# A new order for all steps from the 14th on, in a kernel of a state-space layer and a feed-forward network

## The chip, the cores and the metric

The kernel runs on one core of one Trainium2 chip. The metric is the time of one execution on the device in microseconds (us); lower is better. Unless a text says otherwise, a time is the median of several runs. The engines of a core are TensorE (PE in the profile; its weight loads are a row of their own, PEld), VectorE (DVE), ScalarE (ACT), GpSimd (POOL) and SyncE (SP), whose queue issues nearly all DMAs of this kernel. Each engine works through its own queue of instructions in the order of the program, and waits where an instruction needs what another engine hasn't finished.

## What is computed

A Mamba-2 layer over 4 batches, 8 heads, 768 positions, 32 channels for each head, and 16 states, worked in chunks of 32 positions, followed by an RMS norm and a feed-forward network with a SwiGLU gate on 3072 tokens of 256 channels.

```python
log_a = np.log(np.clip(a, 1e-06, 1.0))
for c in range(nc):                              # chunks of 32 positions
    cum = np.cumsum(la, axis=-1)                 # la: log_a of the chunk
    L = np.exp(cum[:, :, :, None] - cum[:, :, None, :]) * causal
    CB = np.einsum('bhin,bhjn->bhij', Cc, Bc)
    y_intra = np.einsum('bhij,bhjd->bhid', CB * L, xc)
    y_inter = np.einsum('bhin,bhnd->bhid', Cc, state) * np.exp(cum)[:, :, :, None]
    y[:, :, sl] = y_intra + y_inter
    state = decay_full[:, :, None, None] * state + np.sum(Bx, axis=2)
...
x = y.transpose(0, 2, 1, 3).reshape(3072, 256)
xn = x / np.sqrt(np.mean(x * x, axis=-1, keepdims=True) + 1e-06) * rms_g
g, val = xn @ w_gate, xn @ w_val                 # 256 x 1536 each
out = (g * (1.0 / (1.0 + np.exp(-g))) * val) @ w_out     # 1536 x 256
```

All inputs and outputs are 32-bit floats. The kernel takes the chunks in larger steps than the reference (64 or 128 positions), which gives the same sums.

## The kernel before, in words

The 3072 tokens go through in 6 blocks of 512 (two pairs of 256 positions each). For each block the kernel works out the Mamba-2 part, which gives y, then the norm, then the feed-forward part. All of it is cut into some 1,700 small **steps**, and one long string, `order` (from line 1306), lists them. The loop behind it (line 1477 on) takes the steps one by one and calls the function that stands for each. Since each engine runs its queue in program order, the string sets the queue of every engine at once: which matmul PE does next, which sum DVE does next, which transfer SP sends next. Steps of different blocks are interleaved in it, so that PE has products of one block to do while the other engines prepare the next.

A step reads `block:kind.numbers`. Behind a `/` stands the pair of PSUM banks that it takes (0, 1 or 2), behind a `*` a number of filler products for PE. Steps of block 0 have functions of their own (`first_kinds`), the others are found in `kinds` (from line 1280); a kind there can stand for work on a later block than its number says.

Those that matter here:

- `log4`, `la0`, `mid`, `mids`, `r`, `sums`, `exp`: logarithms of a, and the masks of decays L for the first pairs. `exp` runs on ACT, the products of L with B·C (`L.*`, line 638) on DVE.
- `row.k`, `rowe.k` (line 1192), `rowout.k` (line 1185): rows of decays for four chunks. `rowe` takes an exponential on ACT and sends the result to memory (`rowe<-e_sb`, line 1196); `rowout` sends the rows themselves.
- `dT.p` (line 563) fetches those decays from memory, spread over partitions (`dT<-rowe`, line 566), and `Td.p` (line 571) multiplies them on DVE into the transposed C.
- `g.*`, `gg.p` (lines 592 and 599): products of B and C for a pair, which need `Td`. `gg.p/s` takes a PSUM pair s. `A`, `S`: additions to the state and the states. `y.p/s` (lines 705, 714, 734): the outputs of a pair, in a PSUM pair s.
- `yt.p` and `sq.p`: y copied and squared by ACT out of its PSUM pair, which is free for another step after that (lines 824, 827, 789).
- `ms`, `rs`, `xn`, `tx`: the norm, its result xn, and differences of parts of xn.
- `fetch.k` (line 171): one of 18 pieces of the weights, up to 0.5 MB, into one of six buffers. Weights are converted on the way: `pow.k` (line 210, two instructions on ACT), `man.k` (line 221, DVE), `wt.k` (line 227, DVE). A buffer is free again when `pow` and `man` have read it. `fetch.12` and above belong to w_out.
- `early.*` (line 901) and `gate.f` (line 891): gate and value products of block 0 for the first f tiles, done plainly; `silu`, `hid` behind them.
- `P.k.j` (line 977): one product of a scheme that needs 7 products instead of 8 for a 2 × 2 split of the weights and tokens, for the j-th pair of tiles of the 1536 channels; four matmuls each. `take` copies out of PSUM on ACT (line 983), `C` adds on DVE (line 989), `silu` and `hid` follow on ACT and on DVE or POOL.
- `O.k.h` (line 1108): one of 20 products of a similar scheme for the output weights, with its sums `u` (DVE) and `up` (POOL; line 1076) ahead of it and its totals `w` (line 1139 on DVE, or on ACT) behind it. `put`: the result goes out.

ACT holds one set of function tables at a time. `functions(name)` (line 195) emits a load (lines 200 and 202) where the steps, in the order of the string, change from silu to exponential or logarithm or back. The steps `set`, `exps` and `table` do nothing but call it.

The lines that walk the string:

```python
    for step in order.split():
        step, _, slots = step.partition("/")
        blk, _, step = step.partition(":")
        step, _, filler = step.partition("*")
        fillers[:] = [int(filler)] if filler else []
        kind, *numbers = step.split(".")
        picks[:] = map(int, slots)
```

Of the kernel before, what the change touches and what calls it, by code (L numbers as in the profile page):

```python
# [1518 lines left out]
```

## Time and profile before

| | |
|---|---|
| median of 3 runs | 386.6 us (386.2 to 387.43) |
| the profiled execution | 387.79 us |
| its span (first to last instruction) | 386.0 us |
| granted clock of PE | 1.000 |
| HBM read and written | 23.68 MB and 3.74 MB |

The profile is one execution. Its page gives for each engine the busy time, its share of the span, and the number of instructions. The span is a little shorter than the execution's time, since something lies around it. Matmuls are pipelined and their ends are modelled, so a busy PE isn't PE at its peak. A chain of work is followed back from the last instruction to whatever released each step. Waits are listed by the line that waited and the line that released it; a view by windows gives the busy time of each engine in each stretch, and a view in order of time single instructions with what they waited for.

### The profile page before, as it was taken

The page shows a single profiled execution, that of the slowest core. Times are in us where ns is not written, and L with a number is a line of the kernel's source. Part 1 is how long each engine was busy: PE and PEld are TensorE (multiplying, and loading weights), DVE is VectorE, ACT ScalarE, POOL GpSimd, SP SyncE. Part 2 cuts the span into 40 slices and gives each one's busy share as a digit, 9 for nine tenths or more (in the row PEclk, how much of TensorE's full clock was granted, in tenths as well). Part 3 has the DMA queues.
Part 4 walks back from the last instruction along what each step waited for, and adds up shares of the span by engine and source line. Part 5 has one row for each costly group of instructions (what it writes and reads, how often), then busy time and mean ns, then how long its engine had stood idle before and what let it go on. Part 6 is the DMA issues. An engine that isn't in the chain of part 4 may idle for free.

```text
span 386.0 us, 9707 instructions
## 1 busy us (share of the span) xinstructions
PE 379.9 (98%) x3837; PEld 330.1 (85%) x3837; DVE 282.1 (73%) x632; ACT 219.7 (57%) x455; POOL 152.3 (39%) x171
## 2 busy tenths in 40 slices
PE   8999999999999999999999999999999999999997
PEld 5675478889988999888898988899888899888996
DVE  6895979999997989656688566578735677454675
ACT  2778767957698361776571446562474551555410
POOL 5022046536756554553475501463630046112131
PEclk9999999999999999999999999999999999999999
DMA  8888987574127044355134050000100000100001
GB/s 90 226 125 231 325 152 156 159 168 72 11 39 135 10 73 104 54 98 126 34 55 87 15 109 2 1 17 21 56 3 2 0 8 28 56 0 0 2 0 56
DMA packets 110084, 28.04 MB, mean 73 GB/s; under 512 B 94840, under 2 KB 107992, under 8 KB 110040
## 3 DMA queue, kind: packets, MB, share of 16 engines
q1 hardware_dynamic: 107960, 27.30, 33.4%
q8 instruction: 30, 0.49, 0.5%
q10 hardware_dynamic: 2080, 0.13, 0.4%
q14 instruction: 14, 0.11, 0.1%
HBM read 23.68 MB, written 3.74 MB: 71 GB/s over the span
## 4 chain that ended last, share of the span: by engine, by line
PE 92%; DMA 3%; DVE 1%; SPq 1%; ACT 1%; issue 1%; DVEq 0%
PE gate L977 30%; PE o L1108 23%; PE val L977 22%; PE y L734 3%; PE gate L891 3%; PE o L1009 3%; PE g L599 1%; DMA rowe<-e_sb 1%; PE gate L901 1%; DMA dT<-rowe 1%; PE e L460 1%; PE g L592 1%; DMA L<-rowd 1%; SPq L143 0%; PE idle L328 0%
## 5 line engine op out<-in xcount | busy, mean ns | idle before, releaser
L989 DVE TENSOR_TENSOR c<-val,p 128x512 f32<-128x512 f32 x99 | 67.6, 687 | 39.1 <-PE val L977 30.3
L983 ACT COPY p<-gate 128x512 f32<-128x512 f32 x99 | 56.9, 582 | 49.7 <-PE gate L977 46.6
L977 PE MATMUL gate<-tx,wgv 128*128 128x256 f32 x264 | 65.8, 380 | 0.0
L977 PEld LDWEIGHTS gate<-tx,wgv 128*128 128x128 f32 x264 | 49.4, 190 | 6.7 <-ACT p L983 0.2
L1002 POOL TENSOR_TENSOR hid<-c 128x256 f32<-128x256 f32 x31 | 24.3, 795 | 76.4 <-ACT c L208 73.7
L208 ACT ACTIVATE c<-c 128x256 f32<-128x256 f32 x99 | 39.0, 414 | 25.4 <-DVE c L989 25.1
L1108 PE MATMUL o<-two,hid 128*128 128x128 f32 x308 | 42.4, 276 | 0.0
L1139 DVE TENSOR_TENSOR ob<-ob,o 128x128 f32<-128x128 f32 (+1 forms) x116 | 31.1, 295 | 14.0 <-PE o L1108 9.6
L1108 PEld LDWEIGHTS o<-two,hid 128*128 128x128 f32 x308 | 39.1, 192 | 1.1 <-ACT ob L1135 0.2
L1002 DVE TENSOR_TENSOR hid<-c 128x256 f32<-128x256 f32 x68 | 30.1, 455 | 7.9 <-ACT c L208 7.5
L977 PE MATMUL val<-tx,sw 128*128 128x256 f32 x132 | 33.9, 381 | 0.0
L977 PE MATMUL val<-xn,sw 128*128 128x256 f32 x132 | 33.9, 379 | 0.0
L977 PE MATMUL val<-xn,wgv 128*128 128x256 f32 x132 | 33.5, 380 | 0.0
L977 PE MATMUL gate<-xn,wgv 128*128 128x256 f32 x132 | 33.2, 381 | 0.0
L977 PE MATMUL gate<-tx,sw 128*128 128x256 f32 x132 | 33.1, 379 | 0.0
L1076 POOL TENSOR_TENSOR s<-s,hid 128x512 f32<-128x512 f32 (+1 forms) x14 | 18.1, 1291 | 28.3 <-PE o L1108 24.8
L493 POOL TENSOR_SCALAR_AFFINE_SELECT L<-L 64x512 f32<-64x512 f32 x32 | 22.0, 686 | 14.8 <-ACT L L208 13.7
L977 PEld LDWEIGHTS val<-xn,wgv 128*128 128x128 f32 x132 | 24.9, 190 | 3.4
L977 PEld LDWEIGHTS val<-tx,sw 128*128 128x128 f32 x132 | 24.6, 190 | 3.7 <-issue 0.4
L977 PEld LDWEIGHTS gate<-tx,sw 128*128 128x128 f32 x132 | 24.8, 190 | 3.2
L1002 DVE TENSOR_TENSOR hid<-u,gate 128x256 f32<-128x256 f32 x33 | 13.6, 417 | 18.5 <-ACT u L208 18.5
L1076 POOL TENSOR_TENSOR s<-hid 128x512 f32<-128x512 f32 (+1 forms) x15 | 19.6, 1310 | 18.5 <-DVE hid L1002 14.3
(211 smaller groups left out, 729.2 us busy)
## 6 DMA issues: line engine op xcount, KB each, us to landing
L<-rowd SPq DMA_DIRECT2D x32, 128.0 KB, 3.1
xr<-in_x_dram SPq DMA_DIRECT2D x24, 128.0 KB, 3.3
wr<-in_moe_w_out_dram SPq DMA_DIRECT2D x6, 511.5 KB, 5.3
out_dram<-ob SPq DMA_DIRECT2D x23, 128.0 KB, 1.9
wr<-in_moe_w_gate_dram SPq DMA_DIRECT2D x5, 511.5 KB, 4.5
wr<-in_moe_w_val_dram SPq DMA_DIRECT2D x5, 511.5 KB, 5.6
br<-in_B_dram SPq DMA_DIRECT2D x23, 64.0 KB, 3.0
dT<-rowe SPq DMA_DIRECT2D x10, 128.0 KB
```

Source lines behind the costliest of these rows:

```text
L208: nc.scalar.activation(**operands)
L493: nc.gpsimd.affine_select(out=L[r], in_=L[r], pattern=[[0, L.shape[1]], [1, HC]], compare_op=ALU.is_ge, fill=0.0, base=0, channel_multipli ...
L734: nc.tensor.matmul(out=y[2 * k + u][rows, (2 * n + i) * HC:(2 * n + i + 1) * HC], start=(k, u, rows.start) not in opened, stop=True, skip_ ...
L891: nc.tensor.matmul(out=gv[:, k], lhsT=w[:, t, fs], rhs=xns[0][:, t], start=(t == 0), stop=(t == 1))
L977: nc.tensor.matmul(out=dst[:, half[w]], lhsT=lhsT, rhs=rhs, start=(k in (1, 2, 5) and w == 0), stop=True, skip_group_check=True)
L983: nc.scalar.copy(out=t, in_=Xs[j])
L989: nc.vector.tensor_tensor(out=t, in0=Zs[j], in1=a, op=ALU.add)
L1002: engine.tensor_tensor(out=hid[:, 2 * j + c // 10 - 1, c % 10 - 1], in0=u, in1=src[:, half[1]], op=ALU.mult)
L1009: nc.tensor.matmul(out=o, lhsT=hid[:, f, k // 2, (k % 2) * P:(k % 2 + 1) * P], rhs=wo[:, f], start=opens, stop=(f == NF // 2 - 1), skip_gr ...
L1076: engine.tensor_tensor(out=hidden_or_sum(o)[:, g], in0=hidden_or_sum(in0)[:, g], in1=hidden_or_sum(in1)[:, g], op=ALU.add if in1[0] == "+" ...
L1108: nc.tensor.matmul(out=Os[blk, b][:, place * P:(place + 1) * P], lhsT=hidden_or_sum(u)[:, g], rhs=rhs, start=(blk, b) not in opened, stop= ...
L1139: nc.vector.tensor_tensor(out=o, in0=o, in1=src, op=ALU.add if what[0] == "+" else ALU.subtract)
```

## The change

Only the string `order` is another. It holds the same steps, with the same PSUM pairs and fillers; the first 16 are the same, and so are the last seven. In between the new string is a permutation: the lead-in (block 0 up to its first P steps) has another order, and so has the interleaving of every later block. The table loads aren't steps: they follow from the order. In the part below the whole lead-in up to `0:y.3` is shown, then the places of one step, `0:exps`, and the ends.

```diff
     order = """
         0:warm 0:a 0:set 0:bc.0 0:ident 0:bc.1 0:bc2.1.1 0:ones 0:zeros 0:ident16 0:whole 0:kinks
-        0:idle.7 0:gcol 0:x.0 0:never 0:after 0:fetch.0 0:fetch.1 0:x.1 0:whole16 0:mask.0.0/0
-        0:part 0:hmask 0:upto 0:mid 0:mids 0:part2 0:aT 0:mask.1.1/2 0:la0 0:log4.0.4 0:upto2 0:r.0
-        0:fetch.2 0:head 0:sel 0:middles 0:after2 0:fetch.3 0:log4.4.2 0:log4.6.2 0:bc.3 0:tmask
-        0:parts.0 0:log 0:c*2 0:cx 0:mask.0.1/1 0:turn.0 0:Tb.0 0:T.0 0:d 0:dx 0:sums.0.1 0:sums.0.0
-        0:exp.0.1 0:never16 1:exps 0:exp.0.0 0:turn.1 0:scale.1.0 0:scale.1.1 0:last.1 0:cc
-        0:scale.0.0 0:scale.0.1 0:T.1 0:mean 0:g.0.1/1 0:Tt.1.0 0:g.0.0/0 0:Tt.1.1 0:L.0.1 0:L.0.0
-        0:sums.1.1 0:exp.1.1 0:row.1 0:rowout.1 0:man.0 0:bc.2 0:mask.1.0/1 0:sums.1.0 0:rowe.1
-        0:g.1.1/0 0:L.1.1 0:Tl.1 0:g.1.0/2 0:exp.1.0 0:L.1.0 0:fetch.4 0:last.0 0:Tl.0 0:fetch.7
-        0:dT.2 0:tok 0:tokout 0:A.1 0:A.0 0:S.0 0:S.1 0:pow.0 0:wt.0 0:y.0/1 0:sq.0 0:pow.1 0:y.1/2
-        0:sq.1 0:row.0 0:yt.0 0:man.1 0:wt.1 0:mask.3/1 0:rowe.0 0:yt.1 0:ydone.1 0:r.1 0:man.3
-        0:scale.3 0:eps 0:early.0.0/0 0:early.0.1 0:rowout.0 0:ms.0 0:parts.1 0:pow.3 0:pow.2 0:wt.3
-        0:rs.0 0:mask.2/2 0:scale.2 0:man.2 0:wt.2 0:sums.3 0:sums.2 0:exp.3 0:turn.2 0:T.2 0:Tt.2.0
-        0:xn.0 0:turn.3 0:norm.0 0:T.3 0:Tt.3.1 0:Tt.2.1 0:fetch.5 0:Tt.3.0 0:exp.2 0:Td.2
-        0:early.1.0/1 0:early.1.1 0:dT.3 0:man.4 0:table.1 0:x.2 0:norm.1 0:man.5 0:Td.3 0:silu.0
-        0:hid.0 0:pow.4 0:gate.2/0 0:txp.0.0 0:cw.0.0 0:gg.2/1 0:L.2.0 0:wt.4 0:man.7 0:pow.5 0:wt.5
-        0:L1.2.2 0:fetch.8 0:fetch.9 0:silu.2 0:hid.2 0:man.8 0:pow.8 0:wt.8 0:L1.2.3 0:gate.3/2
-        0:pow.7 0:gate.4/1 0:fetch.6 0:man.6 0:A.2 0:txp.0.1 0:silu.3 0:x.3 0:hid.3 0:pow.6
-        0:gate.5/0 0:tx.0.2 0:txp.0.3 0:fetch.11 0:wt.7 0:man.9 0:fetch.10 0:S.2 0:silu.4 0:pow.9
-        0:fetch.12 0:hid.4 0:bc.5 0:wt.6 0:cwp.3.0 0:wt.9 0:silu.5 0:hid.5 0:man.11 0:cw.3.1
-        0:cw.3.2 0:cw.4.0 0:fetch.13 0:silu.1 0:y.2/2 0:S.3 0:x.5 0:cwp.4.1 0:ydone.0 0:switch.1
-        0:P.2.3 0:bc.4 0:x.4 0:switch.0 0:pow.11 0:P.1.3 0:P.1.4 0:take.1.3 0:C.11.3 0:P.2.4 0:P.6.3
-        0:yt.2 0:sq.2 0:gg.3/2 0:take.1.4 0:silug.11.3 0:C.11.4 0:L.3.0 0:take.6.3 0:cwp.3.3 0:P.5.3
-        0:cwp.1.0 0:P.7.3 0:silug.11.4 0:P.6.4 0:take.7.3 0:P.5.4 0:P.4.3 0:hidgp.11.3 0:wt.11
-        0:L1.3.2 0:scale.5 0:L1.3.3 0:cwp.4.2 0:cwp.4.3 0:take.6.4 0:C.22.3 0:P.3.3 0:man.10
-        0:scale.4 0:pow.10 0:wt.10 0:silug.21.3 0:cwp.5.0 0:cwp.5.1 0:hidg.11.4 0:P.7.4 0:take.7.4
-        0:y.3/2 0:C.12.3 0:fetch.15 1:table 0:silug.22.3 0:hid.1 0:P.4.4 0:pow.12 0:silug.21.4
...
-        1:w.21 1:put.2 2:sq2.1.3 2:P.2.1 2:C.11.1 2:L1.3 2:take.6.1 2:P.7.1 2:take.6.0 2:P.7.0
-        2:take.7.0 0:exps 2:P.5.0 2:L1.2 2:C.22.0 2:L 2:P.5.1 2:take.7.1 2:P.4.0 2:silu.21.0
...
-        5:O.14.0 5:O.5.1 5:w.17 5:u.15 5:O.1.0 5:O.1.1 5:O.19.0 5:O.19.1 5:w.12 5:w.19 5:w.24 5:w.23
-        5:put.3 5:put.0 5:put.1 5:O.10.0 5:O.10.1 5:w.25 5:put.2.1 5:O.14.1 5:w.21 5:put.2.0
+        0:idle.7 0:gcol 0:x.0 0:never 0:upto 0:whole16 0:mask.0.0/0 0:x.1 0:fetch.0 0:fetch.3
+        0:fetch.1 0:aT 0:mask.1.1/2 0:part 0:part2 0:head 0:mean 0:mid 0:mids 0:la0 0:upto2 0:hmask
+        0:tmask 0:sel 0:after 0:after2 0:log4.0.4 0:r.0 0:middles 0:parts.0 0:log 0:c*2 0:cx
+        0:mask.0.1/1 0:turn.0 0:Tb.0 0:T.0 0:d 0:dx 0:scale.1.0 0:sums.0.1 0:log4.4.2 0:sums.0.0
+        0:exp.0.1 0:exp.0.0 0:turn.1 0:T.1 0:last.1 0:Tl.1 0:Tt.1.1 0:scale.0.1 0:scale.0.0
+        0:scale.1.1 0:g.0.1/1 0:never16 0:L.0.1 0:sums.1.1 0:g.0.0/0 0:L.0.0 0:cc 0:fetch.2 0:bc.2
+        0:log4.6.2 0:Tt.1.0 0:last.0 0:row.1 0:rowe.1 0:exp.1.1 0:bc.3 0:rowout.1 0:mask.1.0/1
+        0:Tl.0 0:sums.1.0 0:g.1.1/0 0:L.1.1 0:exp.1.0 0:g.1.0/2 0:L.1.0 0:tok 0:tokout 0:A.1 0:A.0
+        0:S.0 0:S.1 0:man.0 0:y.0/1 0:yt.0 0:pow.0 0:wt.0 0:man.3 0:y.1/2 0:yt.1 0:ydone.1 0:sq.0
+        0:pow.3 0:row.0 0:rowe.0 0:sq.1 1:exps 0:eps 0:r.1 0:parts.1 0:early.0.0/0 0:early.0.1
+        0:pow.1 0:fetch.4 0:dT.2 0:rowout.0 0:man.1 0:wt.1 0:fetch.5 0:cw.0.0 0:fetch.7 0:pow.2
+        0:man.2 0:ms.0 0:rs.0 0:xn.0 0:txp.0.0 0:norm.0 0:scale.2 0:wt.2 0:wt.3 0:txp.0.1 0:mask.2/2
+        0:mask.3/1 0:sums.3 0:exp.3 0:sums.2 0:exp.2 0:turn.2 0:T.2 0:Tt.2.0 0:Tt.2.1 1:table
+        0:early.1.0/1 0:turn.3 0:T.3 0:Tt.3.0 0:silu.0 0:Tt.3.1 0:man.4 0:hid.0 0:early.1.1 0:norm.1
+        0:Td.2 0:man.5 0:dT.3 0:Td.3 0:pow.4 0:gate.2/0 0:pow.5 0:wt.4 0:wt.5 0:gg.2/1 0:L.2.0
+        0:L1.2.3 0:scale.3 0:silu.2 0:hid.2 0:fetch.8 0:x.2 0:man.8 0:L1.2.2 0:pow.7 0:silu.1
+        0:pow.8 0:wt.8 0:man.7 0:wt.7 0:gate.3/2 0:silu.3 0:fetch.6 0:pow.6 0:tx.0.2 0:man.6 0:hid.3
+        0:wt.6 0:cwp.3.0 0:A.2 0:S.2 0:gate.4/1 0:fetch.9 0:pow.9 0:silu.4 0:fetch.11 0:pow.11
+        0:cw.3.1 0:hid.4 0:man.9 0:man.11 0:wt.9 0:cwp.1.0 0:cw.4.0 0:cwp.4.2 0:gate.5/0 0:silu.5
+        0:table.1 0:hid.5 0:ydone.0 0:switch.1 0:x.3 0:y.2/2 0:S.3 0:cw.3.2 0:fetch.12 0:pow.12
+        0:yt.2 0:sq2.2.0.0 0:bc.4 0:wt.11 0:fetch.10 0:man.10 0:switch.0 0:P.1.3 0:take.1.3 0:P.1.4
+        0:P.2.3 0:C.11.3 0:txp.0.3 0:sq.2 0:hid.1 0:gg.3/2 0:P.6.3 0:P.2.4 0:silug.11.3 0:take.1.4
+        0:P.5.3 0:take.6.3 0:P.7.3 0:cwp.4.1 0:P.6.4 0:L1.3.3 0:man.12 0:C.11.4 0:P.5.4 0:bc.5 0:x.5
+        0:L1.3.2 0:scale.5 0:scale.4 0:spread.10 0:spread.9 0:sq2.2.1.3 0:spread.11 0:x.4 0:fetch.17
+        0:pow.10 0:wt.10 0:take.7.3 0:P.4.3 0:cwp.3.3 0:C.22.3 0:P.3.3 0:take.6.4 0:P.7.4 0:cwp.5.0
+        0:cwp.5.2 0:hidgp.11.3 0:cwp.5.1 0:L.3.0 0:y.3/2 0:silug.21.3 0:cw.1.1 0:C.12.3 0:silug.12.3
...
+        1:C.22.5 1:hidp.22.4 1:u.0 1:O.15.0 1:silu.11.5 1:hid.11.5 1:P.4.5 1:silu.21.5 1:hid.21.5
+        1:up.3 1:u.1 1:O.2.0 1:O.2.1 1:w.0 0:exps 1:P.3.5 1:C.12.5 1:L1.2 1:L 1:O.15.1 1:O.3.0
+        1:O.3.1 1:silu.12.5 1:hid.12.5 1:up.4 1:up.5 1:up.6 1:O.0.0 1:O.0.1 1:u.9 1:O.16.0 1:w.2
...
+        5:O.1.0 5:O.1.1 5:O.19.0 5:O.19.1 5:w.12 5:w.19 5:w.24 5:w.23 5:put.3 5:put.0 5:put.1
+        5:O.10.0 5:O.10.1 5:w.25 5:put.2.1 5:O.14.1 5:w.21 5:put.2.0
```

More of the change, by code (lines that the diff above doesn't have):

```diff
@@ new lines @@
+        0:put.3 1:T.1.0 0:w.23 1:hid.21.2 1:sq2.0.3 1:sq2.0.1 1:dT.1 0:put.1 2:bc.0 0:O.10 0:w.25
+        1:sq2.0.0 0:put.0 1:sq2.0.2 1:sq2.1.1 0:put.2 1:P.5.2 1:C.22.2 1:P.7.3 1:Tt.1.1 1:g
+        0:table.0 1:take.7.3 1:P.4.3 1:hidp.22.1 1:cwp.2.3 1:P.3.2 1:silu.22.0 1:hidp.22.0
+        1:silu.22.2 1:hidp.22.2 1:silu.21.3 1:C.11.3 0:sub.10 1:hidp.12.1 0:ex.10 1:P.1.4 1:take.1.4
+        1:hid.21.3 1:Td.0 1:C.12.2 0:sub.8 0:ex.8 1:silu.12.2 1:hidp.12.2 1:subp.2 1:Td.1 1:P.5.3
+        1:P.2.4 1:P.6.4 1:take.6.4 1:P.1.5 1:C.11.4 1:silu.11.4 1:take.1.5 1:C.22.3 1:silu.22.3
@@ new lines @@
+        2:C.11.4 2:hid.11.5 2:sub.1 3:Tt.1.0 2:silu.11.4 3:Td.1 2:P.7.5 2:take.7.5 2:P.7.4
+        2:take.7.4 2:P.5.4 2:hid.11.4 2:C.22.4 2:table 2:silu.22.2 2:hid.22.2 2:silu.22.4
+        2:hidp.22.4 2:P.4.5 2:silu.21.5 2:hid.21.5 2:up.1 2:P.4.4 2:silu.21.4 2:hid.21.4 2:yt
+        2:P.5.5 2:C.22.5 2:silu.22.5 2:up.0 2:u.3 2:up.4 2:hid.22.5 2:O.2.0 2:O.2.1 2:O.15.0
+        2:O.15.1 2:P.3.5 2:w.2 2:w.0 2:C.12.5 2:O.3.0 2:O.0.0 2:O.3.1 2:P.3.4 2:O.0.1 2:silu.12.5
+        2:hid.12.5 2:up.5 2:up.6 2:u.2 2:exps 2:ex.1 2:C.12.4 2:w.4 2:w.10 2:u.9 4:dT.1 3:spread.2
@@ new lines @@
+        4:O.10.0 4:O.1.1 4:O.10.1 4:w.25 4:w.17 4:put.3 4:put.0 4:w.21 4:w.14 4:put.2 4:w.23 4:w.19
+        4:put.1 5:P.6.1 4:exps 5:take.6.1 5:P.1.0 5:take.1.0 5:P.2.1 5:C.11.1 5:P.7.1 5:take.7.1
+        5:P.2.0 5:C.11.0 5:P.6.0 5:take.6.0 5:P.4.1 5:P.5.1 5:C.22.1 5:silu.21.1 5:hid.21.1 5:P.5.0
+        5:P.7.0 5:take.7.0 5:silu.11.0 5:P.1.3 5:take.1.3 5:P.3.1 5:C.12.1 5:silu.12.1 5:hidp.12.1
+        5:hid.11.0 5:P.4.0 5:silu.21.0 5:hid.21.0 5:P.6.3 5:take.6.3 5:C.22.0 5:silu.22.0
+        5:silu.11.1 5:hid.22.0 5:P.2.3 5:C.11.3 5:silu.11.3 5:silu.22.1 5:hid.22.1 5:P.1.2
```

258 lines of the change are left out of this document (120 added, 138 removed).

## The prediction

> **What bounds the kernel now.** I read the page's first part, then what TensorE waited for, then the windows of 10 us, and then the chain in order of time where a window was short of 10.
>
> ```profile
> span 386.0 us, 9707 instructions
> ```
>
> ```profile
> PE 379.9 (98%) x3837; PEld 330.1 (85%) x3837; DVE 282.1 (73%) x632; ACT 219.7 (57%) x455; POOL 152.3 (39%) x171
> ```
>
> TensorE (PE) is busy for 379.9 us, 98% of the span. A permutation keeps its matmuls, so only the other 2% are to be won from idle time. The next view, the waits of PE, says where it stood waiting for another engine behind the very start; the columns are total, times and longest, in us.
>
> ```profile
> PE g L599 <- DVE T L573: 0.7, 1, 0.7
> PE y L705 <- DVE S L686: 0.5, 1, 0.5
> PE o L1108 <- POOL s L1076: 0.4, 1, 0.4
> PE y L734 <- DVE L L632: 0.2, 1, 0.2
> ```
>
> They add to 1.8 us. The windows (stretch: length, busy time of PE, PEld, DVE, ACT, POOL with instructions; then PE clock, DMA share, GB/s) put them in their places.
>
> ```profile
> 0.00:10.00 10.00, 8.76 (x55) 5.73 (x57) 6.67 (x31) 3.16 (x8) 5.01 (x17) 1.00 0.81 92
> 10.00:20.00 10.00, 9.35 (x172) 6.38 (x170) 8.75 (x19) 8.02 (x15) 0.00 (x0) 1.00 0.87 234
> 30.00:40.00 10.00, 9.26 (x59) 5.36 (x58) 6.04 (x14) 7.32 (x12) 1.74 (x3) 1.00 0.85 238
> 40.00:50.00 10.00, 10.00 (x124) 4.50 (x126) 8.49 (x21) 7.50 (x12) 1.12 (x1) 1.00 1.02 279
> 120.00:130.00 10.00, 10.00 (x56) 8.99 (x55) 8.91 (x18) 5.09 (x13) 3.53 (x4) 1.00 0.53 73
> 200.00:210.00 10.00, 9.36 (x237) 8.48 (x239) 8.88 (x20) 1.86 (x6) 7.54 (x8) 1.00 0.53 105
> ```
>
> PE loses 1.24 us in the first window (most of it before anything has been loaded, and the first 16 steps are the same in both orders), 0.65 in the second, 0.74 between 30 and 40, and 0.64 between 200 and 210, which is the pair of waits of 0.4 and 0.2. The stretch 40 to 50 is full for PE, but its DMA share is 1.02: transfers queue there. That is all a new order has to work on, apart from new waits of its own. The granted clock is 1.00 in each of these windows.
>
> **The change part by part.** All products, sums, copies and transfers are kept, so I cost only places where PE waits now or would wait next.
>
> *The wait at gg.2 (30 to 40 us).* First the instruction that makes the decays, then the chain behind it (start, duration, what).
>
> ```profile
> 21.80 0.27 ACT L208 ACTIVATE e_sb<-r_ps 128x128 f32<-128x128 f32 x1
> ```
>
> ```profile
> 28.98 4.52 DMA rowe<-e_sb
> ...
> 33.55 3.35 DMA dT<-rowe
> ...
> 37.47 0.65 PE g L599 x20
> 38.13 7.06 PE gate L891 x16
> ```
>
> The decays of rowe.0 are ready at 22.07, but the queue of SyncE (SP) sends them at 28.98, behind fetch.4, fetch.7 and dT.2 among others. Two transfers in a row then bring dT.3 (33.55 + 3.35 = 36.90), VectorE (DVE) multiplies, and the second part of gg.2 starts 0.57 behind the landing, at 37.47. In the new order rowe.0 stands directly behind rowout.1 and ahead of fetch.4, dT.2 and fetch.7, and bc.2 has gone ahead of rowe.1. The cut is at least the stretch from the old fetch.4 to the old rowe.0.
>
> ```profile
> 26.20 0.43 SPq L184 DMA_DIRECT2D wr<-in_moe_w_gate_dram  x1
> ...
> 43.14 0.41 SPq L184 DMA_DIRECT2D wr<-in_moe_w_out_dram  x1
> ```
>
> So rowe.0 goes out 28.98 − 26.20 = 2.8 us earlier, and dT.3 lands near 36.90 − 2.8 = 34.1. PE comes to the second part of gg.2 when gate.2 and the first part are done; it stood waiting 0.74 there, so it wants it at 36.73. With those 0.57 behind the landing the multiplication is done by 34.7, in time by 2 us. **Gain 0.74**, the whole wait, and no more: late next is gate.2 itself.
>
> *The lead-in before it.* The steps from the logarithms to the first states are reordered among themselves. On DVE `head` and `mean` now stand ahead of `la0`, and on ScalarE (ACT) a logarithm, `log4.4.2`, directly ahead of the first mask exponential. By my walk through both queues with the old durations, gate.2 starts 0.2 later. No row shows the new order, so I bound this by the nearest wait that could vanish, and the nearest instruction that could come to stand in front.
>
> ```profile
> 16.02 2.35 DVE L638 TENSOR_TENSOR L<-g,L 128x1024 f32<-128x1024 f32 x2 [0.77 <-PE g L592]
> ```
>
> DVE, whose two mask products per pair set the pace here, idles 0.77 before the second pair: a better order gains up to 0.77. One of those products in the wrong place costs half of the 2.35 for two, 1.18. I take **+0.2 later**, near the middle.
>
> *The new place of gg.3 (50 to 55 us).* The stretch from gg.2 to the end of y.2 keeps its work (three gates, the state additions, y.2), so all of it comes 0.74 − 0.2 = 0.54 earlier. Behind y.2 stood five P steps and then gg.3; now there are three, and two of the five (P.6.3, P.2.4) follow it. gg.3 takes the PSUM pair that y.2 filled, so it waits until ACT has emptied it by yt.2 and sq.2. The chain shows what PE has to cover this with.
>
> ```profile
> 50.70 1.06 PE val L977 x4
> 51.76 1.73 PE gate L977 x8
> 53.48 0.86 PE val L977 x4
> 54.35 0.86 PE gate L977 x4
> 55.21 0.62 PE g L599 x32
> ```
>
> The first of them starts where y.2 ends. Five P steps were 1.06 + 1.73 + 0.86 + 0.86 = 4.51. Three are 1.06 + 0.86 + 0.86 = 2.78, so PE asks for gg.3 at 50.70 − 0.54 + 2.78 = 52.94. ACT's rows for that stretch before:
>
> ```profile
> 49.22 0.60 ACT L208 ACTIVATE u<-gate 128x512 f32<-128x512 f32 x1 [1.99 <-PE gate L891]
> 49.71 0.62 ACT L208 ACTIVATE u<-u 128x512 f32<-128x512 f32 x1
> 50.23 0.77 ACT L208 ACTIVATE e<-wr,kinks 128x512 f32<-128x512 int16 x1
> 51.03 0.72 ACT L208 ACTIVATE e<-e,kinks 128x512 int32<-128x512 f32 x1
> 52.66 0.58 ACT L983 COPY p<-gate 128x512 f32<-128x512 f32 x1 [0.90 <-PE gate L977]
> 53.14 0.44 ACT L824 COPY yt<-y 128x128 f32<-128x128 f32 x2
> ...
> 54.35 0.72 ACT L208 ACTIVATE sq<-y 128x128 f32<-128x128 f32 x3
> ```
>
> The last of these ends at 55.07 and gg.3 starts at 55.21, so already now there is no slack. In the new order ACT has silu.5, pow.12, yt.2, take.1.3, sq.2. silu.5 starts 0.54 earlier at 48.68; the next can start 0.49 behind it (49.71 − 49.22), at 49.17. pow.12 takes 51.03 + 0.72 − 50.23 = 1.52, to 50.69; yt.2 takes 54.35 − 53.14 = 1.21, to 51.90; take.1.3 takes 0.48, to 52.38; sq.2 takes 0.72, to 53.10; and 0.14 later, at 53.24, gg.3 starts. PE waits 53.24 − 52.94 = **0.3**, and every P step behind gg.3 in its queue waits with it.
>
> *Two more table loads.* The instructions are not quite kept: a table load is emitted where the set of functions changes in program order. Followed through both orders, there are 26 before and 28 after: `0:exps` now stands between products of block 1, near 128 us, with a silu soon behind it.
>
> ```profile
> 196.34 1.28 ACT L200 ACT_TABLE_LOAD   x1
> 197.63 0.42 ACT L208 ACTIVATE c<-c 128x256 f32<-128x256 f32 x1
> ```
>
> That is 2 × 1.28 = 2.56 us of ACT, in a window (120 to 130) in which ACT is busy for 5.09 of 10. I cost it at nothing; what hides it is the 4.91 idle, and with that gone it costs up to 2.56. Here a rule speaks against the change. The rows above show the next activation 0.01 us behind the end of the load. The Trainium skill, page "ScalarE: Activation LUTs", section "What ACT_TABLE_LOAD costs", gives 1283 ns for a load, as this trace does, but adds a drain of about 1380 ns; by it the pair would take some 5.3 us of ACT, by estimate 0.4 more than is idle, and the sum would come out 0.4 higher. No drain is seen in these rows behind the load, and I stay with 2.56.
>
> *Blocks 1 to 5.* PE does not wait there except for 0.64 near 205, where exponentials on ACT, POOL's masks and a sum on POOL come together. The same steps stand at that boundary in the new order. I cost it at nothing, bounded by −0.64 and, for as many new waits, +0.64. The last seven steps are the same, so the end behind the last product stays.
>
> *The sum* against the profiled execution, which took 387.79 us with a span of 386.0 (1.8 us lie around it, and it stands 1.2 us over the median of 386.6): −0.74 + 0.2 + 0.3 = −0.24, so 387.55 there, and 386.36 by the median; I say 386.4. A measurement of this kernel can tell about 0.3%, or 1.16 us, from no change: faster means under 385.44, slower over 387.76.
>
> **The rivals.** *First, more is won.* If the lead-in gains its 0.77 where I take a loss of 0.2, ACT is just in time for gg.3, and the new interleaving closes the 0.64 near 205, then −0.74 − 0.77 − 0.64 = −2.15, or **384.45**. For it: every one of these is a wait on one chain that an order can loosen, and nearly all steps of the lead-in have moved. Against it: each needs its own luck, and the lead-in has been walked without finding it.
>
> *Second, ACT blocks behind a fetch; slower.* pow.12 stood far behind y.3 before; now it stands ahead of yt.2 in ACT's queue, and it can't start before fetch.12 has landed. The first rows here are the waits of the SP queue for conversions on ACT, the last the mean time from issue to landing.
>
> ```profile
> SPq L184 <- ACT e L208: 6.5, 5, 2.8
> ```
>
> ```profile
> wr<-in_moe_w_out_dram SPq DMA_DIRECT2D x6, 511.5 KB, 5.3
> ```
>
> With the old issue at 43.14 it lands at 48.4, and ACT wants it at 49.17: 0.7 to spare. But this fetch takes a buffer that a conversion has to release, and such a wait was up to 2.8 us. Then it lands at 51.2, 2.1 late; yt.2, sq.2 and gg.3 are late by as much, and all of PE behind them: 386.36 + 2.1 = **388.4**. The point from which it decides: from a landing at 49.17 on, each us of lateness is a us of PE, and from 49.17 + 1.41 = 50.6 on the kernel is slower than the limit below. For it: the DMA share of 1.02 in just that stretch. Against it: in the new SP queue fetch.12 has gone ahead of fetch.10, so 0.5 MB less is in front of it.
>
> *Third, PE has far more room.* The weight loads (PEld) are busy for 85%, and 15% of 386 us would be 58 us. The trace speaks against it: from 21 us on the P steps follow each other at 0.86 us for four products and never faster, and PE waits only where the list says. If even a tenth of this were open to an order, the time would be **380.8**. The Trainium skill, page "Perfetto Trace Analysis", section "Identifying the Most-Contended Engine", holds that busy time of matmuls misleads and that the share of weight loads measures the headroom; on this kernel the constant pitch disagrees.
>
> *Fourth, the change doesn't quite do what it says.* Table loads and new waits at the block boundaries cost 0.64 at the old boundary's size up to 2.56 if ACT has no cover near 128 us: **387.0 to 388.9**.
>
> **How the numbers follow.** My forecast has 0.42 (of it 0.36 within the limit, 0.03 each beyond it); the first rival 0.29, the second 0.18, the third 0.03, the fourth 0.08 (0.05 within the limit, 0.03 slower). Faster: 0.03 + 0.29 + 0.03 = 0.35. Same: 0.36 + 0.05 = 0.41. Slower: 0.03 + 0.18 + 0.03 = 0.24. The range goes from the first rival's 384.4 to the second's 388.5. As both signs have much of the chance, the forecast's own range: from −0.77 instead of +0.2 in the lead-in to +1.18, which is 385.4 to 387.3.
>
> **What would show it.** In the changed profile: rowe's transfer starting near 26 and not 29, dT.3 landing near 34, and no wait of gg.2 for DVE at L573 (step one); gate.2 near 33.0 (lead-in); the last gate of block 0 ending 0.5 earlier; gg.3 near 53.2 with ACT's sq as its releaser and a wait of 0.3; 28 table loads and no PE wait between 120 and 140. PE's busy time should again be about 380. I am wrong if gg.3 waits for over 1.7 us with pow.12 behind a DMA (second rival), if windows of blocks 1 to 5 show PE under 9.9 in new places (fourth), or if the time falls although the list of waits is the same, which would mean that products ran at another pitch.

## The result, and the profile after

The changed kernel took 388.56 us (median of 7 runs, 388.04 to 390.42) against 386.63 us for the kernel before (7 runs). The measured ratio of the two, which need not be the quotient of the medians (1.0050 here), is 1.0061, with a 95% interval from 1.0039 to 1.0083: slower by more than the 0.3% that a measurement can tell, where 386.4 us and most likely no change was forecast. A second measurement of the same kernel, among the experiments, gave 389.94 us and 1.0083 (1.0062 to 1.0105). Five executions in what follows took 556 to 2205 us, one of them the profiled one of the first experiment (granted clock 0.657); the ratios and the readings of profiles leave them out.

The two strings are the same in their first 16 and their last 28 steps, so the new order begins with the 17th step, and not with the 14th as the title has it.

The profiled execution took 390.1 us. Its page, first and busy part:

```profile
span 388.4 us, 9717 instructions
```

```profile
PE 380.9 (98%) x3837; PEld 330.4 (85%) x3837; DVE 283.8 (73%) x632; ACT 223.4 (58%) x457; POOL 149.4 (38%) x171
```

The span is 2.4 us longer. PE's busy time grew by 1.0 us only, and the products are the same, so most of it is waiting. What PE waited for (total, times, longest, in us):

```profile
PE y L664 <- DMA xr<-in_x_dram: 1.3, 2, 0.8
PE idle L328 <- DVE warm L354: 1.1, 1, 1.1
PE o L1108 <- DVE s L1076: 0.9, 1, 0.9
PE gate L977 <- DVE xn L873: 0.4, 1, 0.4
PE o L1108 <- DVE ob L1139: 0.4, 1, 0.4
PE gate L977 <- DVE hid L924: 0.2, 1, 0.2
```

The wait of `gg.2` (L599 behind DVE, L573) is gone from this profile, as forecast. In its place stand one for a load of x, and three at a block boundary. The windows (columns as in the prediction) show where:

```profile
10.00:20.00 10.00, 9.81 (x168) 7.00 (x170) 8.46 (x19) 7.16 (x14) 0.00 (x0) 1.00 0.92 242
30.00:40.00 10.00, 10.00 (x64) 5.82 (x64) 8.78 (x18) 9.35 (x17) 0.72 (x1) 1.00 0.80 212
...
60.00:70.00 10.00, 8.72 (x181) 6.78 (x180) 7.06 (x19) 5.76 (x16) 5.49 (x7) 1.00 0.90 223
120.00:130.00 10.00, 10.00 (x54) 8.87 (x53) 8.58 (x17) 6.17 (x15) 4.11 (x5) 1.00 0.46 64
190.00:200.00 10.00, 9.12 (x182) 8.21 (x181) 7.60 (x15) 8.10 (x15) 8.09 (x7) 1.00 0.27 60
200.00:210.00 10.00, 9.15 (x74) 8.36 (x72) 8.67 (x16) 2.65 (x8) 5.65 (x7) 1.00 0.21 46
```

30 to 40 is full now (9.26 before). 60 to 70 has lost 1.28, and 190 to 210 has lost 1.73 where it lost 0.64 before.

**The load.** In SP's queue `x.4` now stands behind `spread.10`, `spread.9`, `sq2.2.1.3` and `spread.11`, eight transfers. The chain of the changed kernel in order of time:

```profile
58.41 0.50 SPq L500
...
60.47 3.82 DMA xr<-in_x_dram
64.30 0.04 issue
64.34 0.66 PE y L664 x40
```

The second half of `x.4` is sent at 60.47 and has landed at 64.30. The additions to the states that `y.3` makes for the next two pairs (L664) start there, in the middle of `y.3`, and every P step queues behind them.

**The boundary of blocks 2 and 3.** First before, then after (start, duration, what):

```profile
194.87 1.18 DVE L1076 TENSOR_TENSOR s<-s,hid 128x512 f32<-128x512 f32 x1
...
196.61 0.71 PE L1108 MATMUL o<-wo,hid 128*128 128x128 f32 x4
197.16 0.61 PE L1108 MATMUL o<-sw,s 128*128 128x128 f32 x4
```

```profile
194.33 1.28 ACT L202 ACT_TABLE_LOAD   x1
...
196.46 0.29 DVE L1139 TENSOR_TENSOR ob<-ob,o 128x128 f32<-128x128 f32 x1 [0.48 <-ACT ob L208]
196.66 1.75 DVE L1076 TENSOR_TENSOR s<-s,hid 128x512 f32<-128x512 f32 x1
...
198.55 0.68 PE L1108 MATMUL o<-sw,s 128*128 128x128 f32 x4 [0.88 <-DVE s L1076]
```

The sum `u.9` (DVE, L1076) stood ahead of the totals `w.4` and `w.10`. Now it stands behind them, and `w.10` waits for a copy that ACT makes only behind its table load. So `u.9` ends near 198.4 and not at 196.05, in a kernel that is 1.0 us later here as a whole (`3:g` at 196.47 and 195.47). PE asks for `O.9.0` (`o<-sw,s`) directly behind the products of `3:g`, where the old order had `O.4.0` (`o<-wo,hid`) first, and waits 0.88.

### The profile page after: what moved, and what is told of

The parts are those of the page before. It is cut to its first block, busy times and chain, and to the rows that moved or that the text cites. A ratio compares the mean times of both kernels' runs of the same rounds, so it can differ in the third digit from the quotient of the medians.

```text
span 388.4 us, 9717 instructions
## 1 busy us (share of the span) xinstructions
PE 380.9 (98%) x3837; PEld 330.4 (85%) x3837; DVE 283.8 (73%) x632; ACT 223.4 (58%) x457; POOL 149.4 (38%) x171
## 4 chain that ended last, share of the span: by engine, by line
PE 84%; DVE 5%; DMA 5%; SPq 2%; ACT 1%; issue 1%; POOL 1%; POOLq 0%; DVEq 0%; ACTq 0%
PE gate L977 28%; PE o L1108 23%; PE val L977 21%; PE o L1009 3%; PE y L734 2%; DMA wr<-in_moe_w_gate_dram 2%; DMA wr<-in_moe_w_val_dram 2%; PE g L599 1%; DMA xr<-in_x_dram 1%; PE gate L901 1%; SPq L500 1%; DVE S L688 1%; PE g L592 1%; DVE hid L1076 1%; ACT e L208 1%
## 5 line engine op out<-in xcount | busy, mean ns | idle before, releaser
L989 DVE TENSOR_TENSOR c<-val,p 128x512 f32<-128x512 f32 x99 | 67.2, 686 | 42.9 <-PE val L977 30.6
L977 PE MATMUL gate<-tx,wgv 128*128 128x256 f32 x264 | 65.6, 380 | 0.0
L977 PEld LDWEIGHTS gate<-tx,wgv 128*128 128x128 f32 x264 | 49.4, 190 | 6.8 <-issue 0.2
L1002 POOL TENSOR_TENSOR hid<-c 128x256 f32<-128x256 f32 x31 | 23.7, 771 | 77.8 <-ACT c L208 77.6
L1002 DVE TENSOR_TENSOR hid<-c 128x256 f32<-128x256 f32 x68 | 30.6, 460 | 9.3 <-ACT c L208 9.2
L977 PE MATMUL val<-xn,sw 128*128 128x256 f32 x132 | 34.1, 381 | 0.0
L977 PE MATMUL gate<-xn,wgv 128*128 128x256 f32 x132 | 33.5, 382 | 0.6 <-DVE xn L873 0.4
L977 PE MATMUL val<-tx,sw 128*128 128x256 f32 x132 | 33.4, 379 | 0.0
L977 PE MATMUL val<-xn,wgv 128*128 128x256 f32 x132 | 33.4, 379 | 0.0
L977 PE MATMUL gate<-tx,sw 128*128 128x256 f32 x132 | 32.9, 380 | 0.0
L1076 POOL TENSOR_TENSOR s<-hid 128x512 f32<-128x512 f32 (+1 forms) x15 | 19.7, 1314 | 24.2 <-DVE hid L1002 21.8
L1076 POOL TENSOR_TENSOR s<-s,hid 128x512 f32<-128x512 f32 (+1 forms) x14 | 17.2, 1228 | 28.2 <-PE o L1108 18.9
L977 PEld LDWEIGHTS val<-tx,sw 128*128 128x128 f32 x132 | 24.9, 190 | 3.3
L977 PEld LDWEIGHTS val<-xn,wgv 128*128 128x128 f32 x132 | 24.8, 190 | 3.4
L977 PEld LDWEIGHTS gate<-xn,wgv 128*128 128x128 f32 x132 | 24.3, 190 | 4.0 <-issue 0.6
L977 PEld LDWEIGHTS gate<-tx,sw 128*128 128x128 f32 x132 | 24.5, 190 | 3.2 <-issue 0.2
```

What stands on the lines that cost most here:

```text
L977: nc.tensor.matmul(out=dst[:, half[w]], lhsT=lhsT, rhs=rhs, start=(k in (1, 2, 5) and w == 0), stop=True, skip_group_check=True)
L989: nc.vector.tensor_tensor(out=t, in0=Zs[j], in1=a, op=ALU.add)
L1002: engine.tensor_tensor(out=hid[:, 2 * j + c // 10 - 1, c % 10 - 1], in0=u, in1=src[:, half[1]], op=ALU.mult)
L1076: engine.tensor_tensor(out=hidden_or_sum(o)[:, g], in0=hidden_or_sum(in0)[:, g], in1=hidden_or_sum(in1)[:, g], op=ALU.add if in1[0] == "+" ...
```

## The experiments

A stretch between two marks of PE's timeline turned out to be the best measure: the start of `gate.2` (L891), of `y.2` and `y.3` (L734), of the first output product of block 0 (L1009), of the products `3:g` (L599) and of block 3's `y` (L734). From `y.3` on, a stretch with the same order repeats within 0.1 us from one execution to the next, and mostly within 0.02, unless a transfer is late.

| us | start to gate.2 | to y.2 | to y.3 | to L1009 | 3:g to y |
|---|---|---|---|---|---|
| before | 32.75 | 16.36 | 12.90 | 8.46 | 12.01 |
| before, again | 32.38 | 15.20 | 12.89 | 8.47 | 12.02 |
| before, x.4 late | 32.69 | 15.50 | 12.89 | 9.30 | 12.02 |
| before, u.9 late | 31.89 | 15.20 | 12.89 | 8.46 | 11.85 |
| before, dT early | 32.70 | 20.03 | 12.89 | 8.46 | 12.01 |
| after | 33.07 | 15.26 | 13.13 | 10.17 | 13.67 |
| after, again | 33.20 | 15.96 | 13.10 | 8.64 | 13.65 |
| after, u.9 | 33.37 | 15.20 | 13.11 | 8.67 | 12.19 |
| after, u.9 and x.4 | 32.43 | 15.60 | 13.11 | 8.65 | 12.18 |
| after, u.9 and exps | 33.59 | 15.65 | 13.12 | 8.68 | 12.18 |
| after, O.4 first | 32.37 | 16.92 | 13.11 | 8.73 | 12.27 |
| after, u.9, x.4, dT | 33.41 | 15.20 | 13.12 | 8.65 | 12.18 |

**x.4 at its old place.** `x.4` goes ahead of `spread.10` in the changed order.

```diff
-        0:spread.10 0:spread.9 0:sq2.2.1.3 0:spread.11 0:x.4 0:fetch.17
+        0:x.4 0:spread.10 0:spread.9 0:sq2.2.1.3 0:spread.11 0:fetch.17
```

> The changed order with one step moved: the load x.4 goes ahead of spread.10 in SP's queue, as in the order before. Theory one (half of the loss is PE waiting in the additions of y.3 for x.4, which the new order sends behind four steps with eight transfers; the other half is the boundary of blocks 2 and 3): y.3 starts near 61.5 and the next P step near 63.2, not 64.9; the run is 1.3 to 1.8 us below the changed kernel, about 387.0. Rival (the transfers that now go later, the spreads, become the wait, or the stall only moves): less than 0.5 us below the changed kernel, with a new PE wait behind a transfer between 60 and 110 us. Rival two (not the waits, but other pitches make the loss): no change at all.

It took 389.64 us, 1.0081 (1.0060 to 1.0102) of the kernel before. Nothing was won: this half of theory one falls. Nor did the stall move: the profile with both moves (below) has no wait behind a transfer between 60 and 110 us.

**u.9 at its old place.**

```diff
-        2:exps 2:ex.1 2:C.12.4 2:w.4 2:w.10 2:u.9
+        2:u.9 2:exps 2:ex.1 2:C.12.4 2:w.4 2:w.10
```

> The changed order with one step moved: the sum u.9 of block 2 goes ahead of exps, ex.1, C.12.4, w.4 and w.10, where DVE no longer stands behind two totals that wait for ACT's table load. Theory one: the wait of O.9.0 for this sum near 198.5 (0.9 us) goes, and with DVE 1.8 us ahead there the two waits behind it (0.4 and 0.4) shrink too: 0.9 to 1.7 us below the changed kernel, about 387.2. Rival (DVE is simply full at this boundary): the wait shows up again at w.16, xn or L1 a few us later, and under 0.4 us are won.

387.67 us, 1.0029 (1.0015 to 1.0044): 0.9 us under the first measurement of the changed kernel, 2.3 under the second (by the ratios some 1.2 and 2.1). The stretch from `3:g` to `y` fell from 13.67 to 12.19, by 1.48; the waits for `u.9` and for xn are gone from the list.

**Both.**

> The changed order with both moves, x.4 and u.9. Theory one: the two gains add, since PE bounds all between: 2.2 to 3.3 us below the changed kernel, 385.4 to 386.4, and so level with the kernel before or under it by the 0.6 us that the lead-in of the new order wins. Rival (one wait covers the other): the sum is clearly less than both alone.

387.38 us, 1.0024 (1.0006 to 1.0042). With x.4 only 0.3 us more is won, which is no more than noise. The gain of `u.9` holds; 0.7 us stay unexplained by these two.

**The late x.4, put into the kernel before.** `fetch.15`, `spread.10`, `spread.9`, `sq2.2.1.3`, `spread.11` and `x.4`, in this order, go ahead of `y.3`. So the other five move too, to an earlier place.

> The kernel before with the new order's cost alone: x.4 goes behind fetch.15, spread.10, spread.9, sq2.2.1.3 and spread.11 in SP's queue, all of them ahead of y.3; nothing else moves. Theory one: x.4 is sent near 60 and lands near 64, the additions of y.3 wait for it as in the changed kernel, 0.9 to 1.7 us slower than the kernel before (387.6 to 388.3). Rival (SP's order there does not matter): within 0.4 us of the kernel before.

386.52 us, 1.0011 (0.9989 to 1.0033): no cost on the whole. Its profile has the wait, but smaller, and 9.30 instead of 8.46 us behind `y.3`:

```profile
58.93 5.31 SPq L150 DMA_DIRECT2D xr<-in_x_dram  x4
62.70 1.05 PE L664 MATMUL y<-xr,Bd 64*32 64x64 f32 x56 [0.37 <-DMA xr<-in_x_dram]
```

So the late load is a race between a transfer and PE. It was lost by 1.3 us in the first profile of the changed kernel; the next run and the table show how often.

**The changed kernel once more.**

> The changed kernel itself again, as the measure for the others on the same chip, and for a second profile of it. If the wait of y.3's additions for x.4 (1.3 us in the first profile) is a race that only some executions lose, this profile may show it smaller or not at all, as the profile of the u.9 run did; the wait for u.9 near 198 (0.9 us) should be there again in any case. Median near 388.5.

389.94 us. In this profile `x.4` lands in time (`y.3` to L1009 8.64, not 10.17), and the boundary is slow again (13.65). Of the five profiles in the table with the new lead-in and a late x.4, one lost 1.5 us by it and the others under 0.1. Another wait is there instead: `gg.2` again waits for `dT.3`.

```profile
29.29 0.62 SPq L566 DMA_DIRECT2D dT<-rowe  x1
...
37.04 0.42 DVE L573 TENSOR_TENSOR T<-tp,dT 128x256 f32<-128x256 f32 x1 [0.81 <-DMA dT<-rowe]
...
37.52 0.65 PE L599 MATMUL g<-T 32*64 32x128 f32 x20 [0.34 <-DVE T L573]
```

The transfer left 4 us earlier than in the kernel before (33.55) but is on its way for over 7 us, until 37.0, where it took 3.35.

**The new lead-in with the old rest.** The changed order up to `y.3`, then the remaining steps in their old order.

> The changed order up to y.3, then all the other steps in their old order. Theory one as first stated (the new lead-in wins 0.6 us, the late x.4 costs up to 1.7): 0 to 1.1 us slower than before. Theory two (the wait at gg.2 in the profile of before was an accident of that execution, since the run with only x.4 moved doesn't show it, so there was nothing to win; and x.4 mostly lands in time): within 0.4 us of the kernel before. If it is over 1 us slower, the main loss lies in the lead-in and not behind it.

389.05 us, 1.0053 (1.0036 to 1.0071). The cut has its own price: behind `y.3` PE waits 1.0 us for sums that came late (L977 behind DVE, L989), and the stretch from L1009 to `1:g` is 43.90 instead of 41.89. Without these 2.0 us some 387.0 is left. A cut in mid-block measures itself too.

**The old lead-in with the new rest, u.9 mended.**

> The old order up to y.3, then the new order of all that is left, with u.9 at its old place in front of exps of block 2. Theory two says that u.9 was the one large loss of the new order behind the lead-in: within 0.4 us of the kernel before. Rival: the extra table loads near 128 us or another boundary cost something that no list of PE waits shows: 0.5 to 1 us slower than before, as much as the changed kernel with u.9 moved was (0.7 to 1.0).

389.6 us, 1.0063 (1.0041 to 1.0084), with an own price again: 12.05 instead of 8.65 from `y.3` to L1009. Of these 3.4 us, 1.8 are PE waiting for `hid` (L977 behind L1002). The rest is a lower clock right behind that wait; the column in front of the last two is the granted clock.

```profile
64.45 1.79 PE L977 MATMUL gate<-xn,wgv 128*128 128x256 f32 x4 [1.83 <-DVE hid L1002]
```

```profile
60.00:65.00 5.00, 3.17 (x150) 2.53 (x150) 5.00 (x9) 2.72 (x5) 4.07 (x5) 0.98 0.82 237
65.00:70.00 5.00, 5.00 (x17) 4.08 (x17) 4.48 (x14) 2.81 (x10) 1.73 (x3) 0.68 0.65 160
```

Of the clock 0.02 × 5 + 0.32 × 5 = 1.7 us are missing there. The four longest of the seven executions, this one among them, have a mean clock of 0.996, the others 1.000. Without the 3.4 us some 386.2 is left, but that is a subtraction. By itself the run settles nothing.

**The two table loads.** The changed order with `u.9` mended and `0:exps` back behind `2:take.7.0`, which makes 26 loads of the 28.

> The changed order with u.9 moved as before, and also 0:exps moved back to its old place behind take.7.0 of block 2, so that the two extra table loads near 128 us are gone. My prediction's costing (ACT has cover there): no change beside the run with u.9 alone, 387.7. Rival (the loads of 2.6 us reach PE or DVE): 0.4 to 2 us below it.

387.88 us, 1.0034 (1.0019 to 1.0049), against 387.67 and 1.0029 with the loads: no difference. The stretches around 128 us are equal to 0.01 us. The loads in the changed kernel:

```profile
130.37 1.28 ACT L202 ACT_TABLE_LOAD   x1
131.65 1.28 ACT L200 ACT_TABLE_LOAD   x1
132.95 0.42 ACT L208 ACTIVATE c<-c 128x256 f32<-128x256 f32 x1
```

The pair and what follows take 132.95 − 130.37 = 2.58 us, as costed. By the Trainium skill, page "ScalarE: Activation LUTs", section "What ACT_TABLE_LOAD costs", each switch would take about 2.66 with a drain; these rows show no room for one.

**A cleaner cut.** At `1:g`, near 112 us, six steps of each order stand on the other side of the cut in the other. New up to there (with x.4 early), then old:

> The changed order (with x.4 early) up to the step 1:g near 112 us, then all other steps in the old order; only six steps stand on the other side of this cut in the one order and in the other. Theory three (in the profiles so far the time from the start to y.3 was 62.0, 61.1 and 60.8 us with the old lead-in, and 61.5, 62.3, 61.7, 61.1, 62.4 and 61.0 with the new one; the medians say that the old one is mostly near 60.8, so the new one loses on the whole): 0.5 to 1.1 us slower than the kernel before, 387.1 to 387.7. Rival (the prediction's sum: the new lead-in wins 0.2 to 0.6): 386.0 to 386.4. Third (no difference): 386.6.

390.08 us, 1.0099 (1.0080 to 1.0118). And old up to there, then new with `u.9` mended:

> The old order up to 1:g, then the new order with u.9 at its old place. In the profiles the stretches behind 1:g add up to 270.6 us in the new order with u.9 moved, and to 270.8 in the old order: theory three says 0.2 us faster than before, 386.2 to 386.6. Rival (the remaining loss of the new order with u.9 mended, 1 us, lies behind 1:g): 387.3 to 387.7.

387.42 us, 1.0031 (1.0019 to 1.0044). Even this cut isn't free: from `1:g` to `2:g` it takes 32.63 in the first and 31.56 in the second, where both whole orders take 30.3. Taken off, with the second's 0.43 ahead of `1:g`, that leaves 387.7 for the new lead-in with the old rest, and 385.7 for the reverse. It points to the lead-in for the 0.7 to 1 us that is left, but such a subtraction is an argument and not a measurement.

**u.9 late in the kernel before.**

```diff
-        2:u.9 2:exps 2:ex.1 2:w.4 2:w.10
+        2:exps 2:ex.1 2:w.4 2:w.10 2:u.9
```

> The kernel before with only the sum u.9 of block 2 moved behind exps, ex.1, w.4 and w.10. If DVE's lateness alone makes the loss at this boundary, 1.2 to 1.7 us slower than before (387.8 to 388.3). If it takes the new order of PE as well (which asks for O.9.0 directly behind the products of 3:g, where the old order has O.4.0 first), the O.4.0 of four matmuls covers about 0.4 us of it: 0.6 to 1.1 us slower.

386.19 us, 1.0002 (0.9988 to 1.0015): it costs nothing at all, and the stretch is even 0.16 shorter (11.85).

```profile
193.54 1.75 DVE L1076 TENSOR_TENSOR s<-s,hid 128x512 f32<-128x512 f32 x1
194.24 1.28 ACT L200 ACT_TABLE_LOAD   x1
...
194.51 0.71 PE L1108 MATMUL o<-wo,hid 128*128 128x128 f32 x4
...
195.35 0.71 PE L1108 MATMUL o<-sw,s 128*128 128x128 f32 x4
```

The sum is as slow and as late as in the changed kernel, but PE has `O.4.0` to do first and stands for some 0.4 us only; the wait for POOL (0.4) further on then has gone.

**The other half: PE's order.** The changed kernel with `O.4.0` and `O.4.1` ahead of `O.9.0`, u.9 still late.

```diff
-        3:g 2:O.9.0 2:O.17.0 2:O.6.0 2:O.9.1 2:u.10 2:O.4.0 2:O.4.1
+        3:g 2:O.4.0 2:O.4.1 2:O.9.0 2:O.17.0 2:O.6.0 2:O.9.1 2:u.10
```

> The changed kernel with O.4.0 and O.4.1 of block 2 directly behind 3:g on PE, ahead of O.9.0; u.9 stays late on DVE. These eight matmuls take 0.9 us and need nothing that is late, so the 0.9 us of waiting for u.9 is covered. If that wait is the cost: 0.6 to 0.9 us below the changed kernel (389.4 over its twelve runs). If DVE's queue being 1.8 us late is the cost, the other two waits behind it (0.4 and 0.4) grow by as much and less than 0.4 us is won.

388.19 us, 1.0046 (1.0027 to 1.0064), 1.2 under the 12 runs of the changed kernel, though its profile waits 1.3 us at `gg.2`. The stretch from `3:g` to `y` is 12.27. So it takes both: late sum and early demand 13.66, either alone 11.85 to 12.27, neither 12.01.

**dT.3 ahead of two fetches.** The changed order with `u.9` and `x.4` mended, and `dT.3` ahead of `fetch.5` and `fetch.7` in SP's queue.

> The changed order with x.4 and u.9 mended, and with the transfer dT.3 ahead of fetch.5 and fetch.7 in SP's queue. Theory three (dT.3 leaves 3 to 5 us earlier than in the old order but is 7 to 8 us on its way behind those fetches, so gg.2 still waits for it in half of the profiles, 0.4 to 1.7 us): the profile shows no wait of gg.2 for DVE at L573, dT.3 lands within 5 us of its issue, and the median falls by 0.2 to 0.6 below the run with x.4 and u.9 (387.4). Rival (the transfers are slow whatever stands in front): the wait stays and nothing is won.

386.71 us, 1.0012 (0.9996 to 1.0027), against 387.38 and 1.0024 (1.0006 to 1.0042) without it. These intervals overlap, and two measurements of one kernel can differ by as much (below), so the gain is not shown by the times. The profile has no wait of `gg.2`: `dT.3` is issued at 28.64, and the last update of its semaphore stands at 33.62 in the trace, 5.0 us later and not 7.7. With three steps moved, the changed order can't be told from the kernel before.

**gg.3 back behind five P steps, on top of it.**

> As the run with dT.3 early, and with gg.3 behind five P steps instead of three, as in the old order. The stretch from y.2 to y.3 was 13.11 to 13.13 us in every profile with three, and 12.89 to 12.90 with five, so it should be 12.9 here, and the median 0.2 lower than with dT.3 alone, near the kernel before: 386.6 to 387.0.

387.31 us, 1.0014 (0.9989 to 1.0039). Nothing won in the time. The stretch from `y.2` to `y.3` stayed at 13.09, and the next fell from 8.65 to 8.46. With three P steps, the weight load of `gg.3` waits for `sq.2`; with five, the first P step waits for `hid` instead (first the run with `u.9` alone, then this one):

```profile
53.08 0.46 PEld L599 LDWEIGHTS g<-T 32*64 32x64 f32 x32 [0.55 <-ACT sq L208]
```

```profile
50.64 1.59 PEld L977 LDWEIGHTS gate<-xn,wgv 128*128 128x128 f32 x8 [0.28 <-DVE hid L924]
```

`gg.2` waited 1.0 in this profile, and not for `dT.3`:

```profile
36.48 0.43 DVE L224 TENSOR_SCALAR m<-wr 128x512 int32<-128x512 uint32 x1 [1.45 <-DMA wr<-in_moe_w_val_dram]
36.82 0.42 DVE L573 TENSOR_TENSOR T<-tp,dT 128x256 f32<-128x256 f32 x1
```

`man.5` stands ahead of `Td.3` on DVE and waits for `fetch.5`, which this order sends behind `dT.3`. The run before has the same steps up to there and did not wait, so this is a race too.

**The same idea in the kernel before.** `rowe.0` ahead of `fetch.4`, `dT.2`, `dT.3`, `fetch.7`.

> The kernel before with rowe.0 ahead of fetch.4, dT.2 and fetch.7 in SP's queue, and dT.3 directly behind dT.2. If the wait of gg.2 of 0.74 us in the first profile is typical of the kernel before, 0.5 to 0.8 us faster: 385.8 to 386.1. If it belongs to that execution (gate.2 to y.2 took 15.20 in three of five profiles with the old lead-in, which is the time without a wait), 0 to 0.3 us faster, which cannot be told from no change.

390.22 us, 1.0096 (1.0060 to 1.0133): slower, by 1.4 us or more in each of the six executions. `dT` goes early, but `fetch.5` goes later, and again DVE stands behind `man.5`:

```profile
38.59 0.43 DVE L224 TENSOR_SCALAR m<-wr 128x512 int32<-128x512 uint32 x1 [2.92 <-DMA wr<-in_moe_w_val_dram]
...
39.41 0.65 PE L599 MATMUL g<-T 32*64 32x128 f32 x20 [2.71 <-DVE T L573]
```

Behind this wait the granted clock is down again, by 0.34 × 5 = 1.7 us:

```profile
40.00:45.00 5.00, 5.00 (x10) 2.20 (x9) 4.86 (x11) 3.51 (x6) 0.00 (x0) 0.66 1.13 333
```

So wait and clock make 4.4 of the 4.8 us by which the stretch from `gate.2` to `y.2` is longer than 15.20. The three longest of the six executions, this one among them, have the mean clock of 0.996.

**The kernel before once more.**

> The kernel before once more, for a second profile of it and to see how far a kernel differs from itself: within 0.2 us of the others' runs of it. If the first profile was one of its slower executions, this one spans 384.3 to 385.3 us instead of 386.0, and y.3 starts near 60.8 instead of 62.0, with a smaller wait of gg.2 or none.

387.04 us against 386.48 of the same kernel beside it, 1.0014 (1.0000 to 1.0027): two measurements of one kernel differ by 0.56 us. The profile spans 384.9 us, and `gg.2` does not wait:

```profile
span 384.9 us, 9707 instructions
```

```profile
31.36 0.60 SPq L566 DMA_DIRECT2D dT<-rowe  x1
...
34.62 0.42 DVE L573 TENSOR_TENSOR T<-tp,dT 128x256 f32<-128x256 f32 x1 [0.41 <-DMA dT<-rowe]
35.91 0.69 PE L599 MATMUL g<-T 32*64 32x128 f32 x32
```

## Why the prediction was wrong

The step that failed is the one that put blocks 1 to 5 at nothing, "bounded by −0.64 and, for as many new waits, +0.64". The runs showed 1.65 us at the boundary of blocks 2 and 3 in its place, from a sum that came late on DVE and was asked for early by PE. Term by term:

- **gg.2, gain 0.74: wrong, because there was nothing to gain.** The wait was real in the one execution profiled before, and gone in the one profiled after. But of six profiles with the old lead-in (four in the table, and the two runs with the old lead-in and new rest) four take 15.20 from `gate.2` to `y.2`, which is the time without a wait. The prediction noted that its execution was 1.2 us slower than the median, and then took a wait of just that execution as the kernel's own. The new order also failed to remove it: in four of its eight profiles (six in the table, and the two with the old rest; the run with `dT` early left out) the stretch is 0.4 us or more over 15.20. `dT.3` leaves earlier but travels behind two fetches; in three of these four the profile names its transfer as what DVE waited for, in the fourth (`O.4` first) ACT. "dT.3 lands near 34.1" assumed that a transfer takes as long wherever it is queued.
- **Lead-in, +0.2: not refuted and not shown.** `gate.2` starts at 32.4 on the mean of the six old profiles (31.9 to 32.8) and at 32.9 on the mean of the eight new ones (32.3 to 33.6). The ranges overlap, so +0.5 can't be told from +0.2. Which step of it costs something was not tried.
- **gg.3, +0.3 for ACT: right in the mechanism, and nearly in size (0.22).** In eight of the nine profiles with the new lead-in and `gg.3` behind three P steps, its weight load (PEld) stands 0.52 to 0.55 us until `sq.2` is done, 0.2 longer than the 0.33 of the kernel before. Only in the profile after, the first P step had already lost those 0.2 to `hid` (DVE, L924), and `gg.3` at 52.87 follows directly on `sq.2` (52.79). With `gg.3` back behind five P steps the wait for `hid` takes its place, and only the 0.2 of the stretch behind `y.3` are won.
- **Table loads at nothing: right,** shown by removing them.
- **Blocks 1 to 5 at nothing, bounded by 0.64: this is the step that decided.** The boundary of blocks 2 and 3 costs 1.65 more, in both profiles of the changed kernel, and one moved sum takes 1.48 of it away. "The same steps stand at that boundary" was true of the set and not of the order in it: on DVE a sum moved behind two totals that wait for ACT, and on PE the product that needs it moved forward. Against that, the way from `1:g` to the end of the last product without this stretch is 258.41 us in the profile after and 258.81 before (258.43 and 259.12 in the second profiles).
- **x.4: not costed.** It was moved past eight transfers in SP's queue and appears nowhere in the sum. It cost 1.5 in the one of five profiles that lost the race; moved back, it won 0.3 in one pair of runs, within the noise.
- **The rivals.** The first did not come out. The second names 388.4, next to the measured 388.56, by chance: `pow.12` started at 48.93, directly behind `silu.5`, without a wait. A queue did stand behind a fetch, but elsewhere, `man.5` on DVE in two of the experiments. (The landing time of 5.3 us that it reads as a mean is the page's median.) The third is not borne out: PEld is at 85% in both, and the time went up. (The P steps that it starts at 21 us start at 50.6.) The fourth came out in half: there are new waits at a block boundary, its sign of PE under 9.9 in a new place is there (9.12 between 190 and 200), and the time lies in its 387.0 to 388.9. But the upper end of that range came from the table loads, which cost nothing, and the boundary waits stood in it with 0.64 and not 1.65.

Summed up for a typical execution: +1.65 at the boundary, +0.4 at `y.3` and just behind, −0.4 in the other stretches, +0.6 up to `y.2`, and +0.3 for x.4 (one loss of 1.5 in five) make +2.5, between the 1.9 and the 3.4 that the medians of the two measurements give (2.4 and 3.2 by the ratios). The boundary's part is shown by experiments. The part up to `y.2` rests on means over scattered profiles and stays open.

## What to carry to other kernels

When an order is permuted, cost each pair of producer and consumer whose distance changed on both queues: here neither the late sum nor the early demand cost anything alone. Before counting a wait on a DMA as a gain, see it in a second execution, above all when the profiled one is slower than the median. A transfer that is moved forward delays what it overtakes, and the wait comes back on any queue where a conversion of that data stands ahead of the critical instruction.
